# A fused attention and gated feed-forward kernel: k and q of half the batches turned by DMA transposes kept apart from the loads, unread matmuls in TensorE's first waits, and a new plan

## The chip, the cores and the metric

One core of one Trainium2 chip runs the whole program. The metric is the device time of one execution in microseconds (us). Each ratio below is between runs of the kernel before and a changed kernel on the same chip, in alternating rounds. Where two changed kernels from different rounds are compared by their medians, the chips differ too; the kernel before had 213.25 to 213.92 us in all of these rounds. Runs that the record marks as slow are named where they matter. In this kernel TensorE does the matmuls and writes them into PSUM, VectorE and ScalarE copy and compute elementwise, and GpSimd and SyncE issue the DMA transfers.

## The reference, cut to what matters

```python
batch, n_heads, seq, head_dim, n_pack = 8, 8, 576, 64, 32
p_packed = sm_attn(p, k, v)               # 32 packed queries attend over 576 keys
out      = sm_attn(q, p_packed, p_packed) # 576 queries attend over the 32 packed rows
x = out.transpose(0, 2, 1, 3).reshape(8 * 576, 512)
result = (((x @ w1) * (x @ w2)) @ w3) @ w_out      # float32, 4608 x 512
```

k and q come from memory with the sequence along partitions. Both attention steps contract over the head dimension, so k and q have to be turned. Of each batch there are 96 x 3072 values of k, of q and of v in fp16 after the load (589,824 bytes each).

## The kernel before: the parts that matter

The kernel is a list of operations. Each has the engines that may run it, an estimated duration and a priority. A list scheduler inside the kernel simulates the engines with these estimates and writes a fixed instruction order for each engine. On the chip each engine works through its own queue in that order, and semaphores only make it wait. An operation whose data comes later holds up whatever stands behind it on the same engine.

```python
def schedule(plan):
    ...
        dur = op.engines[e]
        if isinstance(dur, tuple):            # a DMA: time to issue, time to move
            issue, trans = dur
            free[e] = t + issue
            begin = max(free["DMA"], t + issue + 0.9)
            if begin < 11.0:
                trans *= 1.35
            free["DMA"] = begin + trans
            done[op], on[op] = begin + trans + LAG, "DMA"
    ...
    order.sort(key=lambda op: (start[op], op.n))
```

k and q are turned by TensorE, 24 transposes of 96x128 for one batch's k and 24 for its q, and two evictions of 128x1152 out of PSUM for each:

```python
def turned(which):
    ...
    for g in range(2):
        ps = Psum(2)
        for u in range(2):
            def fn(e, g=g, u=u, ps=ps):
                ...
                for hc in range(6):
                    ...
                    env.nc.tensor.transpose(t[:, u, SC*hc : SC*hc+SC], s[0:SC, h, 128*c3 : 128*c3+128], env.ident[0:SC, 0:SC])
        ...  # one copy to kT or qT by VectorE or ScalarE
```

v is copied by VectorE into a tile with a column of ones (`va`). All loads are issued from GpSimd's queue and are cast from float32 to fp16 on the way; the output is stored from SyncE's queue. kin, vin, qin, kT and qT have two buffers each, so batch b+2 reuses what batch b has finished with.

The softmax here doesn't subtract the row's maximum and nothing guards it: scores larger than these inputs give would overflow.

## Time and profile before

| | before |
|---|---|
| device time, median of 3 | 213.55 us (213.32 to 214.28) |
| span in the profile | 212.7 us |
| TensorE busy | 195.0 us, 92% |
| first matmul, last matmul ends | 9.02 us, 207.5 us |
| loads into SBUF, stores | 19.66 MB, 9.44 MB |
| loads arrive until about | 100 us, at some 200 GB/s; the last two, k7 and q7, are issued only at 111 and 137 us |

The prediction below shows the lines of the profile. "Granted clock" there is the share of its full clock that TensorE was given. "DMA share" is the time that the packets took, over the time of the core's 16 DMA engines; it passes 1 where packets overlap.

### The profile page before, as it was taken

To read this page: it belongs to the slowest core of one execution; us is meant where nothing else is said; L and a number is where in the kernel's file an instruction comes from. 1 tells how busy PE (TensorE), PEld (TensorE's weight loads), DVE (VectorE), ACT (ScalarE), POOL (GpSimd) and SP (SyncE) were. 2 spreads that over 40 slices of the span, in tenths; PEclk is the share of its full clock that TensorE was granted. 3 is DMA by queue.
4 is the path that set the end of the run, shared out by engine and by line. 5 is a ranking of instruction groups with operands and counts; after the bars stand their busy time and mean duration, and the time that the engine had idled before them with its cause. 6 is when DMAs were issued, how large, how long until landed. Compare 5 with 4: busy or idle time off the path is not lost.

```text
span 212.7 us, 6124 instructions
## 1 busy us (share of the span) xinstructions
PE 195.0 (92%) x2656; PEld 131.5 (62%) x2656; DVE 116.0 (55%) x188; ACT 137.0 (64%) x209; POOL 32.9 (15%) x49
## 2 busy tenths in 40 slices
PE   0188989999999999999999999999999999999990
PEld 0168878667567748785457766757755646776440
DVE  4015434367867776587946845447485665555100
ACT  2154749865798476986899555797858567555321
POOL 7742245511131112111000000100000000000000
PEclk9999999999999999999999999999999999999997
DMA  5999999999999999999829203192013313103353
GB/s 68 185 193 202 206 203 200 197 203 204 205 241 230 224 204 249 203 212 205 177 53 150 62 0 103 49 167 80 20 23 82 99 52 99 54 13 86 99 151 101
DMA packets 34124, 29.51 MB, mean 139 GB/s; under 512 B 3888, under 2 KB 28464, under 8 KB 34096
## 3 DMA queue, kind: packets, MB, share of 16 engines
q0 software_dynamic: 28336, 19.66, 62.7%
q1 hardware_dynamic: 5760, 9.44, 15.4%
q8 instruction: 21, 0.34, 0.6%
q14 instruction: 7, 0.06, 0.1%
HBM read 39.32 MB, written 9.44 MB: 229 GB/s over the span
## 4 chain that ended last, share of the span: by engine, by line
PE 89%; DMA 3%; ACT 2%; DVE 2%; issue 1%; POOL 0%; DVEq 0%; ACTq 0%; POOLq 0%
PE ps L585 29%; PE pb L624 29%; PE pb L365 8%; PE ps L412 7%; PE ps L557 5%; DMA ab<-in_moe_w_dram 3%; PE pb L445 2%; PE pb L468 2%; PE ps L534 2%; PE ps L624 2%; PE ps L514 2%; PE pb L347 1%; ACT ab L357 1%; PE ps L445 1%; DVE pT L334 1%
## 5 line engine op out<-in xcount | busy, mean ns | idle before, releaser
L585 PE MATMUL ps<-a,G 128*128 128x288 f16 x512 | 70.8, 286 | 0.2
L624 PE MATMUL pb<-wc,ab 128*128 128x512 bf16 x272 | 68.7, 380 | 0.0
L601 DVE TENSOR_TENSOR ab<-ps,bs 128x576 bf16<-128x576 f32 x64 | 48.2, 755 | 30.7 <-ACT bs L597 25.1
L585 PEld LDWEIGHTS <-G 128*128 128x128 f16 x512 | 48.5, 98 | 17.0 <-issue 0.9
L597 ACT CAST bs<-ps 128x576 bf16<-128x576 f32 x64 | 40.9, 639 | 26.5 <-PE ps L585 26.0
L624 PEld LDWEIGHTS <-ab 128*128 128x128 bf16 x288 | 25.8, 98 | 25.1 <-issue 2.7
L572 ACT CAST G<-ps 128x1024 f16<-128x1024 f32 x20 | 19.8, 1015 | 4.6 <-PE ps L557 4.4
L637 DVE COPY o<-pb 128x512 f32<-128x512 f32 x15 | 10.4, 691 | 20.7 <-PE pb L624 11.0
L639 ACT COPY o<-pb 128x512 f32<-128x512 f32 x19 | 11.1, 585 | 15.3 <-PE pb L624 15.0
L365 PE MATMUL pb<-wo,ab 128*128 128x256 f16 x128 | 16.7, 286 | 2.3 <-ACT ab L357 1.4
L570 DVE CAST G<-ps 128x1024 f16<-128x1024 f32 x12 | 14.4, 1221 | 3.2 <-PE ps L557 2.9
L365 PEld LDWEIGHTS <-ab 128*128 128x128 f16 x128 | 12.5, 102 | 5.2 <-ACT ab L357 2.7
L347 PE MATMUL pb<-ident,ab 128*128 128x128 f16 x48 | 4.8, 266 | 9.0 <-DMA ab<-in_moe_w_dram 9.0
L278 POOL DMA_DIRECT2D qin<-in_q_dram x8 | 6.2, 772 | 40.2 <-PE ps L412 34.2
L427 ACT COPY qT<-ps 128x1152 f16<-128x1152 f16 x9 | 10.0, 1117 | 3.4 <-PE ps L412 3.2
L540 ACT ACTIVATE ln<-ps 128x576 f32<-128x576 f32 x16 | 10.1, 650 | 2.7 <-PE ps L534 2.5
L557 PE MATMUL ps<-w,ppT 64*32 64x256 f16 x512 | 10.9, 272 | 0.1
L544 ACT ACTIVATE ri<-ln 128x576 f16<-128x576 f32 x16 | 10.7, 687 | 0.3
L456 ACT ACTIVATE es<-pb 96x512 f16<-96x512 f32 x18 | 10.4, 594 | 0.6
L347 PEld LDWEIGHTS <-ab 128*128 128x128 f16 x64 | 4.9, 116 | 9.4 <-DMA ab<-in_moe_w_dram 9.0
L357 ACT COPY ab<-pb 128x1024 f16<-128x1024 f16 x5 | 5.0, 1016 | 8.5 <-PE pb L347 8.5
L412 PE MATMUL ps<-ident,kin 96*128 96x96 f16 x192 | 10.3, 206 | 0.0
(56 smaller groups left out, 185.1 us busy)
## 6 DMA issues: line engine op xcount, KB each, us to landing
kin<-in_k_dram POOLq DMA_DIRECT2D x8, 576.0 KB, 13.6
vin<-in_v_dram POOLq DMA_DIRECT2D x8, 576.0 KB, 15.5
qin<-in_q_dram POOLq DMA_DIRECT2D x8, 576.0 KB, 15.5
out_dram<-o SPq DMA_DIRECT2D x24, 192.0 KB, 2.5
out_dram<-o SPq DMA_DIRECT2D x24, 128.0 KB, 2.4
ab<-in_moe_w_dram POOLq DMA_DIRECT2D x8, 256.0 KB, 10.2
w<-in_moe_w_dram POOLq DMA_DIRECT2D x8, 256.0 KB, 12.2
out_dram<-o SPq DMA_DIRECT2D x24, 64.0 KB, 2.2
```

Source lines behind the costliest of these rows:

```text
L347: env.nc.tensor.transpose(t[:, 128 * ct : 128 * ct + 128], env.w3[:, ci, 128 * ct : 128 * ct + 128], env.ident[:, :])
L365: env.nc.tensor.matmul(pv(ps)[:, 0:256], env.w3T[:, ci, 128 * ct : 128 * ct + 128], env.wo[:, h, ct, :], start=(ct == 0), stop=(ct == DFC ...
L412: env.nc.tensor.transpose(t[:, u, SC * hc : SC * hc + SC], s[0:SC, h, 128 * c3 : 128 * c3 + 128], env.ident[0:SC, 0:SC],)
L544: env.nc.scalar.activation(out=env.ri[g][:, :, :], in_=env.ln[g][:, :, :], func=AF.Exp, scale=-1.0)
L557: env.nc.tensor.matmul(pv(ps)[32 * hp : 32 * hp + 32, g, 256 * w : 256 * w + 256], env.ppT[b % 2][64 * g : 64 * g + 64, g, 32 * hp : 32 * ...
L570: env.nc.vector.tensor_copy(o, pv(ps))
L572: env.nc.scalar.copy(out=o, in_=pv(ps))
L585: env.nc.tensor.matmul(pv(ps)[:, half, 0:HS], env.G[b % 2][:, mc // 2, g, w, 128 * (mc % 2) : 128 * (mc % 2) + 128], env.a2[b % 2][:, g, h ...
L597: env.nc.scalar.copy(out=env.bs[bs][:, :, :], in_=pv(ps)[:, :, 0:HS])
L601: env.nc.vector.tensor_mul(env.ab(pair)[:, mc, b % 2, :].rearrange("p (a s) -> p a s", a=2), pv(ps)[:, :, 0:HS], env.bs[bs][:, :, :],)
L624: env.nc.tensor.matmul(pv(ps), ab[:, ic, 128 * t : 128 * t + 128], env.wc[:, ic, :], start=(ic == 0), stop=(ic == DFC - 1),)
L639: env.nc.scalar.copy(out=env.o[ob][:, :], in_=pv(ps))
```

## The change

The intent is to take 192 transposes (k and q of batches 4 to 7) from TensorE, which is the bound, to the DMA engines by `dma_start_transpose` on SyncE's queue. A list called `order` lays the loads and these transposes in groups, and semaphores make each group wait for the group ahead of it, so that a transpose never runs beside a load. Unread matmuls (their result is never used) on a small tile fill TensorE's waits up to 20 us so that its clock is at full rate when the first data come; the first loads come in another order; the planner's DMA estimates are new; and the priorities were searched again.

```diff
+    turn="k4 q4 k5 q5 k6 q6 k7 q7",
+    order="q2 k2 v2 k3 v3 q3 k4 q4 Tk4 Tq4 v4 k5 q5 Tk5 v5 k6 Tq5 q6 q7 Tk6 Tq6 v6 k7 v7 Tq7 Tk7",
+    warm=True,
-    T0=59.57,
+    T0=57.073,
     ... (the other priorities, also new)
-    loads="wo0 w33 w37 w36 pp w30 k_0 w34 wo1 v_0 q_0 w31 w35 k_1 ww0 w32 ww1 ww3 ww2 v_1 q_1",
+    loads="w37 pp w33 wo0 k_0 w36 wo1 w35 w34 w30 q_0 v_0 w31 w32 k_1 ww0 ww1 ww2 ww3 q_1 v_1",
 ...
-            issue, trans = dur
+            issue, lead, trans = dur
 ...                                    # planner: a load of k, q or v is now 2.9 us, a store 0.7, a transpose 2.7
+            if e == "PE" and warm and FILL_END > t > free[e] + FILL + 0.2:
+                ...                     # put groups of 8 unread matmuls where TensorE would wait
 ...
-            if by_dma:
+            if f"{which}{b}" in conf["turn"]:
                 def fn(e):
                     ...
-                    env.nc.sync.dma_start_transpose(
+                    return env.nc.sync.dma_start_transpose(
 ...
+    for i, name in enumerate(names):    # names from conf["order"]
+        if name[0] == "T":
+            gate_on = since_load        # a transpose waits for the loads since the last transposes
+        else:
+            gate_on = since_turn        # a load waits for the transposes since the last loads
+        op.gates = list(gate_on)
 ...
+            for p in getattr(op, "gates", ()):
+                tc.add_manual_dep(made[op].ins, made[p].ins.name, ..., reason="transposes apart from loads")
```

More of the change, by code (lines that the diff above doesn't have):

```diff
@@ L22 @@
 CONF = dict(
-    dma_from=8,
-    P=25.15,
-    T0=59.57,
-    lead=1.32,
-    at=dict(kT=-0.8, va=-0.14, s1=0.87, pv=0.59, ppT=-0.87, qT=-0.07, s2=0.43, z=0.51, G=0.14),
-    G_w=-0.01,
-    tg=[-30.99, -12.45, -0.15, 8.05, -11.49, -2.63, 7.81, -7.38, -17.47, 4.27],
-    ta=[-60.59, -5.81, -1.16, 6.18, -17.56, 4.69, -5.65, -11.68],
-    proj_off=0.87,
-    proj_w=0.98,
-    gate_w=0.03,
-    loads="wo0 w33 w37 w36 pp w30 k_0 w34 wo1 v_0 q_0 w31 w35 k_1 ww0 w32 ww1 ww3 ww2 v_1 q_1",
-    fold0=57.8,
-    fold1=3.02,
-    fold_w=3.51,
+    turn="k4 q4 k5 q5 k6 q6 k7 q7",
+    order="q2 k2 v2 k3 v3 q3 k4 q4 Tk4 Tq4 v4 k5 q5 Tk5 v5 k6 Tq5 q6 q7 Tk6 Tq6 v6 k7 v7 Tq7 Tk7",
+    warm=True,
+    P=25.1631,
+    T0=57.073,
+    lead=1.32,
+    at=dict(kT=-0.7408, va=-0.0681, s1=0.8793, pv=0.6033, ppT=-0.8967, qT=-0.1259, s2=0.3666, z=0.1937, G=0.1798),
+    G_w=0.0315,
+    tg=[-30.3628, -12.7069, -0.7448, 10.1275, -10.7998, -3.047, 4.5158, -7.7837, -17.0459, 6.4814],
+    ta=[-63.315, -4.0378, -0.4914, 4.9319, -18.4481, 6.6318, -9.5115, -11.1072],
+    proj_off=1.003,
+    proj_w=0.9994,
+    gate_w=0.1772,
+    loads="w37 pp w33 wo0 k_0 w36 wo1 w35 w34 w30 q_0 v_0 w31 w32 k_1 ww0 ww1 ww2 ww3 q_1 v_1",
+    fold0=58.7503,
+    fold1=-0.2625,
+    fold_w=4.1191,
 )
@@ L101 @@
 BEGIN, DMA_BEGIN, LAG = 1.27, 2.6, 0.6
+FILL, FILL_END, WARM_AT = 0.44, 20.0, 6.5
 def latency(a, b):
@@ L109, in latency, with schedule @@
     return LATENCY.get((a, b), 0.08)
-def schedule(plan):
+def schedule(plan, warm=CONF["warm"]):
     ops = plan.ops
@@ L146, in schedule @@
             push(op)
-    order = []
+    order, fills = [], []
     n_left = len(ops)
@@ L180, in schedule @@
         if isinstance(dur, tuple):
-            issue, trans = dur
-            free[e] = t + issue
-            begin = max(free["DMA"], t + issue + 0.9)
-            if begin < 11.0:
-                trans *= 1.35
+            issue, lead, trans = dur
+            begin = max(free["DMA"], t + lead)
+            if free["DMA"] == DMA_BEGIN:
+                trans += 1.5
+            elif begin > free["DMA"] + 0.5:
+                trans += 1.0
             free["DMA"] = begin + trans
+            free[e] = max(t + issue, begin + trans - 1.0) if e == "SP" and issue > 2 else t + issue
             done[op], on[op] = begin + trans + LAG, "DMA"
         else:
-            if e == "PE" and t < 4.0:
+            cold = e == "PE" and t < (WARM_AT if warm else 15.5)
+            if e == "PE" and warm and FILL_END > t > free[e] + FILL + 0.2:
+                spare = [i for i in range(len(slots) - 1, -1, -1) if slots[i] <= free[e]]
+                n = int((t - free[e] - 0.2) / (FILL * 2 if cold else FILL))
+                if spare and n:
+                    f = Op(op.n, "fill", {"PE": FILL}, plan.fill, 0.0, Psum(1))
+                    f.alloc.at, f.engine, f.repeat = spare[0], "PE", n
+                    start[f], done[f] = free[e], free[e] + n * FILL * (2 if cold else 1)
+                    fills.append(f)
+            if cold:
                 dur *= 2
@@ L204, in schedule @@
                 push(s)
+    order += fills
     order.sort(key=lambda op: (start[op], op.n))
@@ L219, in build_plan, with dma @@
     Ta = [T0 + P * (b - conf["lead"]) + d for b, d in enumerate(conf["ta"])]
-    rate = 0.199e6
-    def dma(nbytes, issue=0.77):
-        return (issue, nbytes / rate)
+    def dma(issue, trans):
+        return (issue, issue + 0.75, trans)
     def pv(p, n=512, dtype=FP32):
@@ L235, in build_plan, with load @@
     seq = [0]
-    def load(name, nbytes, fn, w, r=()):
+    def load(name, cost, fn, w, r=()):
         seq[0] += 1
-        return add("ld " + name, {"POOL": dma(nbytes)}, fn, -1000 + seq[0], w=w, r=r)
+        return add("ld " + name, {"POOL": cost}, fn, -1000 + seq[0], w=w, r=r)
     def load_w3(j):
@@ L243, in fn @@
             env.nc.gpsimd.dma_start(out=env.w3[:, j, :], in_=env.moe_w3[128 * j : 128 * j + 128, :])
-        load(f"w3 {j}", 128 * 1024 * 2, fn, [("w3", j)])
+        load(f"w3 {j}", dma(0.56, 1.25), fn, [("w3", j)])
     def load_wo(h):
@@ L251, in fn @@
             )
-        load(f"wo {h}", 1024 * 256 * 2, fn, [("wo", h)])
+        load(f"wo {h}", dma(1.0, 2.66), fn, [("wo", h)])
     def load_w12(qd):
@@ L260, in fn @@
                 )
-            load(f"w{w + 1} {qd}", 512 * 256 * 2, fn, [("w12", w, qd)])
+            load(f"w{w + 1} {qd}", dma(0.76, 1.34), fn, [("w12", w, qd)])
     def load_p():
@@ L269, in load_p @@
         seq[0] += 1
-        add("ld p", {"POOL": (1.16, 1.46)}, fn, -1000 + seq[0], w=[("pnat",)])
+        add("ld p", {"POOL": dma(1.17, 1.65)}, fn, -1000 + seq[0], w=[("pnat",)])
     def load_in(which, b):
@@ L277, in fn @@
             x = (env.k, env.v, env.q)[src]
-            env.nc.gpsimd.dma_start(
+            return env.nc.gpsimd.dma_start(
                 out=t[0:SC, :, :], in_=x[b].rearrange("h (p c) d -> p h (c d)", c=CK)
             )
-        load(f"{which}{b}", 96 * 3072 * 2, fn, [(which + "in", b % 2)])
+        load(f"{which}{b}", dma(0.78, 2.9), fn, [(which + "in", b % 2)])
     def emit_loads(names):
@@ L299, in consts @@
         nc = env.nc
-        nc.vector.memset(env.pT[:, :, :, :], 0.0)
         nc.vector.memset(env.blk[:, :], 0.0)
@@ L303, in consts @@
             nc.vector.memset(env.blk[32 * hp : 32 * hp + 32, 32 * hp : 32 * hp + 32], 1.0)
+        nc.vector.memset(env.pT[:, :, :, :], 0.0)
         for t in env.vaug:
@@ L387, in attention @@
     def attention(b):
-        by_dma = b >= conf["dma_from"]
         def turned(which):
@@ L401, in fn @@
                     )
-                add(f"{dst} {b}", {"SP": (1.0, 4.0)}, fn, att(b, dst) - 5, r=[(raw, b % 2)], w=keys)
+                add(f"T {which}{b}", {"SP": (2.9, 1.0, 2.7)}, fn, att(b, dst) - 5, r=[(raw, b % 2)], w=keys)
                 return
@@ L648, in fn @@
                     )
-            add(f"st {pair} {t}", {"SP": (0.3, 0.7)}, fn, vt + 0.9 * width / len(tiles), r=[("o", ob)])
+            add(f"st {pair} {t}", {"SP": (0.8, 1.0, 0.7)}, fn, vt + 0.9 * width / len(tiles), r=[("o", ob)])
     def rows_of(t, pair):
@@ L673, in build_plan, with fill @@
             project(pair, range(4, 9), Tg[b + 1], P * conf["proj_w"])
+    by_name = {op.name: op for op in plan.ops}
+    names = [("T " if x[0] == "T" else "ld ") + x.lstrip("T") for x in conf["order"].split()]
+    since_load, since_turn = [], []
+    last = None
+    for i, name in enumerate(names):
+        op = by_name[name]
+        if name[0] == "T":
+            if last != "T":
+                since_turn = []
+            gate_on = since_load
+            since_turn.append(op)
+        else:
+            op.vt = i - 500
+            if last == "T":
+                since_load = []
+            gate_on = since_turn
+            since_load.append(op)
+        last = name[0]
+        op.gates = list(gate_on)
+        for p in gate_on:
+            if p not in op.preds:
+                op.preds.add(p)
+                p.succs.append(op)
+    def fill(e):
+        for i in range(8):
+            env.nc.tensor.matmul(pv(fill.ps)[:, 0:128], env.blk[:, :], env.blk[:, :], start=True, stop=True)
+    plan.fill = fill
     return plan
@@ L765 @@
     )
+    made = {}
     for op in order:
-        if op not in first:
-            op.fn(op.engine)
+        if op.name == "fill":
+            op.fn.ps = op.alloc
+            for _ in range(op.repeat):
+                op.fn(op.engine)
+        elif op not in first:
+            made[op] = op.fn(op.engine)
+            for p in getattr(op, "gates", ()):
+                tc.add_manual_dep(
+                    made[op].ins,
+                    made[p].ins.name,
+                    mybir.DependencyInfo(mybir.DependencyClass.Sync, mybir.DependencyReason.DATA),
+                    reason="transposes apart from loads",
+                )
 _INS = ['q', 'k', 'v', 'p', 'moe_w1', 'moe_w2', 'moe_w3', 'moe_w_out']
```

## The prediction

> **What bounds the kernel now.** I read the page's busy shares first, then its chain that ended last, then the busy time by stretch, then TensorE's first 24 us instruction by instruction, and last the groups that the change removes.
>
> ```profile
> PE 195.0 (92%) x2656; PEld 131.5 (62%) x2656; DVE 116.0 (55%) x188; ACT 137.0 (64%) x209; POOL 32.9 (15%) x49
> ...
> PE 89%; DMA 3%; ACT 2%; DVE 2%; issue 1%; POOL 0%; DVEq 0%; ACTq 0%; POOLq 0%
> PE ps L585 29%; PE pb L624 29%; PE pb L365 8%; PE ps L412 7%; PE ps L557 5%; DMA ab<-in_moe_w_dram 3%; PE pb L445 2%; PE pb L468 2%; PE ps L534 2%; PE ps L624 2%; PE ps L514 2%; PE pb L347 1%; ACT ab L357 1%; PE ps L445 1%; DVE pT L334 1%
> ```
>
> TensorE is busy 92% of the span and is 89% of the chain. The transposes of k and q (L412) are 7% of the chain: 0.073 x 212.7 = 15.5 us for 384 of them. They are real TensorE time, not time beside something else. The next view says where TensorE's slack lies (busy time of TensorE by stretch, with clock, DMA share, GB/s):
>
> ```profile
> 0.00:9.02 9.02, 0.00 (x1) 1.00 0.79 115
> 9.02:19.26 10.24, 8.22 (x73) 1.00 1.45 196
> 19.26:50.00 30.74, 29.35 (x443) 1.00 1.34 202
> 50.00:207.50 157.50, 157.39 (x2144) 1.00 0.65 125
> ```
>
> From 50 to 207.5 us TensorE has no idle time (157.39 of 157.50). All idle time is early: 9.02 us before the first matmul, 2.02 us up to 19.26, 1.39 us up to 50. So two things can shorten the program: taking TensorE work out of the full stretch, which should count one for one, and a better start.
>
> ```profile
> 9.02 1.03 PE L347 MATMUL pb<-ident,ab 128*128 128x128 f16 x8 [9.02 <-DMA ab<-in_moe_w_dram]
> 11.16 1.89 PE L365 MATMUL pb<-wo,ab 128*128 128x256 f16 x8 [1.10 <-ACT ab L357]
> 12.84 1.91 PE L347 MATMUL pb<-ident,ab 128*128 128x128 f16 x16
> 15.00 2.25 PE L365 MATMUL pb<-wo,ab 128*128 128x256 f16 x16 [0.25 <-ACT ab L357]
> 17.09 0.61 PE L329 MATMUL pb<-ident,G 128*128 128x128 f16 x8
> 17.54 0.61 PE L347 MATMUL ps<-ident,ab 128*128 128x128 f16 x8
> ...
> 19.26 1.04 PE L365 MATMUL pb<-wo,ab 128*128 128x256 f16 x8 [0.66 <-DVE pT L334]
> ```
>
> The reader is to see the same instruction groups at two speeds. Eight transposes of w3 take 1.03 us at 9.02 and 0.61 us at 17.54; eight fold matmuls take 1.89 us at 11.16 and 1.04 us at 19.26. TensorE runs at half rate until about 15.6 us, although the granted clock is printed as 1.00 here: in this stretch the durations decide.
>
> **What the Trainium skill says.** "TensorE: Matmul & The Clock Gate", Part 1: The HAM clock gate: the default is half clock, and some 3.4 us of sustained activity releases it; 128 columns then go from 107 to 56 ns. The trace agrees on the sizes: (1.03 - 0.61) / 7 gaps is 60 ns by which the spacing shrinks. It took 6.6 us here, since the first matmuls have gaps of 1 us between them. The same page, Part 4: PE-mode transpose, says that transposes do not release the clock. The trace shows transposes at full rate once it is released (0.61 us for eight), and cannot say more; that the fill in the change is ordinary matmuls is the safe choice.
> "DMA: Bandwidth & Descriptors", Latency and other measured facts: a DMA transpose moves 261 GB/s, 350 to 400 in the contiguous case. "VectorE: DVE Perf Modes", The three transpose paths: one 128x128 transpose by DMA takes 1309 ns, by TensorE 390. These two give very different answers for a transpose of 96 x 3072 (24 blocks): 589,824 bytes / 261 GB/s = 2.3 us, or 24 x 1.309 = 31 us. No DMA transpose is in the trace of before, so it can't choose. I take the first, since the second looks like one small transfer with its fixed cost.
>
> **The change part by part.**
> (1) Removed on TensorE: k and q of four batches, 4 x 2 x 24 = 192 transposes.
>
> ```profile
> L412 PE MATMUL ps<-ident,kin 96*128 96x96 f16 x192 | 10.3, 206 | 0.0
> L412 PE MATMUL ps<-ident,qin 96*128 96x96 f16 x192 | 10.3, 206 | 0.0
> ```
>
> The 206 ns is the latency of one; they overlap. The chain of waits has them as "1.02 us x24", so 42.5 ns each on the path. 192 x 42.5 ns = 8.16 us. Of these all but a little lie after 75 us, where TensorE is never idle. Value: -8.2 us.
>
> (2) Removed on ScalarE and VectorE: 16 evictions of 128x1152 out of PSUM, at 1118 ns (ScalarE) or 756 ns (VectorE). Between 75 and 100 us ScalarE is busy 19.79 and VectorE 17.87 of 25 us, so neither was the bound. Value on the path: 0, some slack, and two-bank PSUM slots that come free sooner.
>
> (3) The start. The first load becomes one w3 block (262 kB) in place of half of w_out (524 kB) with a w3 block behind it. In the trace the loads brought 60 GB/s in the first 5 us and 188 GB/s in the next five, so the first 786 kB had been moved at 5 + (0.786 - 0.30) / 0.188 = 7.6 us, and the first matmul's data landed at 8.97, 1.4 us later. 262 kB are moved at about 4.8 us and land by the same distance at 6.2 us: the first useful matmul comes 2.8 us sooner. From there the loads set the pace until about 19 us. By the new order I get p at 7.6, the second w3 at 9.0, wo0 at 11.7, k0 at 14.8, w36 at 16.1 and wo1 at 18.7 us. The work that these make possible by 19.3 us is, at full clock: transposes of three w3 blocks 3 x 0.45, of p 0.9, three fold groups 2.94, k0's transposes 1.02, its scores 0.7, and 0.6 us of what wo1 opens: 7.5 us. Before, TensorE had done 8.22 us busy minus the cold excess (0.42 + 0.85 + 0.85 + 0.33 = 2.44 us from the rows above) = 5.8 us by that time. Difference: 1.7 us; after 19.3 us more work lies ready than before, so some of the 1.39 us of idle time there should go too. The unread matmuls serve this: they run where TensorE would wait, so at full rate they cost nothing, and they release the clock before the first real data. Without them much of the 2.44 us would return. They stop at 20 us. I count -2.0 us.
>
> (4) Added: eight DMA transposes on SyncE's queue. Each: 2.3 us of moving at the skill's rate plus about 2.2 us from issue to landing, which is what the smallest stores here take: an estimate of 4 to 4.5 us. None is on TensorE, so what matters is whether each lands in time. The gates make one chain of loads and transposes. k4 and q4 land when 13.8 MB are in, at about 200 GB/s and a start at 4.5 us: 73 us. Tk4 and Tq4: 81. v4, k5, q5 (8.9 us at that rate, 2 us latency): 92. Tk5 97. v5, k6: 105. Tq5 109. q6, q7: 117. Tk6, Tq6: 126. v6, k7, v7: 137. Tq7, Tk7: 146. Before, the scores of batch 7 began at 163.8 us; with some 10 us gained they should begin near 153. So the last has about 7 us of slack, the earlier ones 10 or more (scores of 6: 148 before, about 138 after, Tk6 122). Value: 0, if a transpose costs under some 5 us.
>
> (5) The gated loads leave holes in the DMA queues, and the stores share SyncE's queue with the transposes: small waits at most. I allow +0.4 us for new waits of this sort.
>
> Sum: 213.55 - 8.2 - 2.0 + 0.4 = 203.75 us; I say 203.5.
>
> **The rivals.**
> A. The transposes are slow. At 8 us each the chain above ends 30 us later, at about 176: TensorE runs out of other work and the time is near 225. At 31 us each it would be above 340. For: the 1309 ns figure, and that the planner had this path switched off before. Against: the bandwidth figure, and that the change plans each transpose in as few microseconds as a load. At 6 us each: 8 us of the slack are passed by some, about 206 to 210.
> B. Stores stuck behind a waiting transpose. SyncE issues in order; four output tiles are buffered. A transpose that waits 10 us for loads holds the stores, the output copies stop, a PSUM bank stays taken and TensorE stalls. For: the projections come in runs of a tile each 1.8 us around 55 to 60 us. Against: SyncE waited 121.1 us on ScalarE and 45.0 on VectorE, so it is idle most of the time, and over the span a tile comes each 4 us. If it bites: +1 to +4 us, so 204 to 207.
> C. The start gains nothing, as the loads are the limit there (share 1.45, 196 GB/s). Then only the removed work counts: 205.4.
> D. ScalarE or VectorE takes over as the bound in the denser stretch. They have 21% and 29% to spare between 75 and 100 us and lose work of their own, TensorE shrinks by 5%: I give it little; +1 us.
>
> **The range and the chances.** Sum 203.5; C alone gives 205.4, B or D some more; the start at its best (the earlier landing of 2.8 us and much of the cold excess, together 4.5 us) gives 201. So 8 times in 10 it lies between 200.5 and 207.0. Within 2% starts at 209.3, which needs rival A or several others together: faster 0.92, same 0.05, slower 0.03.
>
> **What would show it right or wrong.** (1) L412 has 192 matmuls instead of 384 and TensorE's busy time without the unread ones falls by about 8 us. (3) The first w3 transposes start near 6.2 us and take 0.6 us for eight. (4) A transpose takes 4 to 4.5 us from issue to landing, and no wait of TensorE on it is listed beyond a microsecond. (5) The stretch from 50 us to TensorE's end still has no idle time. The end after the last matmul stays 5.2 us. I am wrong if TensorE waits for kT or qT from a DMA, for output copies behind SyncE, or if the first matmul still waits until 9 us.

## The result, and the profile after

| | before | changed |
|---|---|---|
| device time, median of 4 | 213.92 us (213.32 to 214.89) | 222.15 us (220.72 to 223.17) |
| ratio | 1 | 1.0376, 95% interval 1.0302 to 1.0449 |
| span in the profile | 212.7 us | 220.0 us |
| mean granted TensorE clock | 0.994 | 0.977 |
| last matmul ends | 207.5 us | 215.7 us |

A ratio is the mean time of one kernel's runs over the mean of the other's runs in the same rounds, so it is not quite the ratio of the medians. Executions over 1.5% slower than the fastest of the same kernel are left out of the means. The result is correct; it is 3.8% slower where I had said 5% faster.

The page of the changed kernel, its busy shares and the chain of work that ended last (the line numbers have moved: L585 is now L597, L624 is L636, L601 is L613):

```profile
PE 197.2 (90%) x2568; PEld 131.2 (60%) x2568; DVE 111.3 (51%) x181; ACT 128.3 (58%) x200; POOL 33.0 (15%) x49
...
DMA 46%; PE 42%; POOL 3%; DVE 3%; issue 3%; ACT 1%; SPq 0%; POOLq 0%; ACTq 0%; DVEq 0%
```

The chain was 89% TensorE and 3% DMA; now it is 46% DMA. TensorE's busy 197.2 us contain 8.20 us of unread matmuls and, as is shown below, some 4.7 us (an estimate) by which half rate stretched its work, so its real work did shrink. What grew is waiting. Busy time of TensorE by stretch in the changed kernel (length, busy with count, granted clock, DMA share, GB/s):

```profile
0.00:20.00 20.00, 15.49 (x221) 1.00 1.13 153
20.00:50.00 30.00, 28.03 (x409) 1.00 1.33 202
50.00:75.00 25.00, 22.70 (x412) 1.00 1.29 222
75.00:100.00 25.00, 23.56 (x393) 1.00 0.91 165
100.00:125.00 25.00, 21.74 (x279) 0.86 0.78 147
125.00:150.00 25.00, 25.00 (x255) 1.00 0.87 161
150.00:175.00 25.00, 19.91 (x299) 0.93 0.96 160
```

The same stretches before have 8.96, 28.61, 25.00, 25.00, 24.89, 25.00 and 25.00 us busy. None of the removed transposes lies before 75 us in the kernel before (TensorE has done 144 of 384 by then, those of batches 4 to 7 being the last 192), so the sums up to there can be compared. Two things are to be seen. From 75 to 175 us the changed kernel idles 9.8 us (1.44 + 3.26 + 0 + 5.09), and twice the clock is below 1 in the stretch where it idles. And by 75 us, before the first DMA transpose is issued at 78 us, it is already behind: 66.2 us busy minus 8.2 unread is 58.0 us of work, while before has 62.6 us minus its cold excess of 2.4, which is 60.1.

The start itself looks as I had described it. TensorE's first instructions in the changed kernel (start, duration):

```profile
1.52 4.14 PE L714 MATMUL pb<-blk 128*128 128x128 f16 x40 [1.52 <-DVE blk L316]
5.50 0.61 PE L361 MATMUL pb<-ident,ab 128*128 128x128 f16 x8
...
8.73 1.07 PE L343 MATMUL pb<-ident,G 128*128 128x128 f16 x16 [1.73 <-DVE G L330]
...
12.52 1.91 PE L379 MATMUL pb<-wo,ab 128*128 128x256 f16 x16 [0.50 <-DMA wo<-in_moe_w_out_dram]
```

The first useful matmul is at 5.50 us instead of 9.02, and eight transposes take 0.61 us, the full rate. Still, by 20 us only 15.49 - 8.20 = 7.3 us of real work are done, 0.8 us more than before (8.96 - 2.44 = 6.5).

TensorE's two long waits are the longest ones of these two rows (who waited for whom, us in total, times, longest us; `ab` is VectorE's gate product, `va` its copy of v):

```profile
PE ps L597 <- DVE ab L613: 5.4, 4, 3.3
PE pb L480 <- DVE va L445: 3.9, 1, 3.9
```

Where the first of them comes from is in the chain between 89 and 127 us, in order of time (start, duration, what):

```profile
89.39 13.38 DMA qin<-in_q_dram
...
102.91 6.41 DMA kT<-kin
...
109.90 7.11 DMA vin<-in_v_dram
...
117.03 0.04 DVE va L445
...
117.90 0.76 DVE ab L613
...
118.70 1.12 PE ps L597 x4
119.82 0.43 PE pb L457 x8
120.25 2.88 PE ps L597 x12
```

Read it from the bottom. TensorE's gate matmuls start at 118.70, released by VectorE's gate product (`ab`), which frees their PSUM slot. The product had to wait behind the copy of v (`va`), which stands ahead of it in VectorE's queue; the copy waited for v5; v5 was issued only when the transpose of k5 had landed; and that one waited for the burst v4, k5, q5. In one line each, from who waited for whom (us in total, times, longest us), first the changed kernel:

```profile
DVE va L445 <- DMA vin<-in_v_dram: 12.6, 6, 4.3
```

and the kernel before:

```profile
DVE va L433 <- DMA vin<-in_v_dram: 0.7, 2, 0.4
```

The last line of the chain, 12 matmuls in 2.88 us where 12 take 1.47 us elsewhere, shows a second cost. Busy times and granted clock in a narrow stretch just after that wait (the columns are TensorE, its weight loads, VectorE, ScalarE, GpSimd, clock, DMA share, GB/s):

```profile
122.10:123.20 1.10, 1.10 (x17) 0.45 (x19) 0.76 (x1) 0.03 (x1) 0.00 (x0) 0.50 0.00 0
```

In stretches of 0.2 and 0.3 us the clock is 0.50 from 117.8 to 124.7 us, beginning within the wait of 3.26 us (115.44 to 118.70), and from 158.8 to 162.2 us, beginning 1.4 us after the end of the wait of 3.95 us (153.44 to 157.39). TensorE works at half rate for 6.0 and 3.4 us of these, and half of that, about 4.7 us, is an estimate of what it loses. So a long wait costs more than its own length. In the other runs too, each wait of 3.0 us or more after the start (3.02 and 5.99 us in after_nofill, 3.56 and 5.35 in v_ahead, 4.02 in turns_free) brings 3.4 or 6.8 us of half rate, and no shorter one does; the longest of those is 2.12 us, in tuned_gated.

With this the two traces can be balanced. Up to the last matmul (207.5 and 215.7 us), time without real work, idle or filled with unread matmuls, grew from 12.5 to 26.7 us (+14.2). Half rate took 4.7 us where the cold start had taken 2.4 (+2.3). What is left for the real work at full rate is 8.3 us less, as foretold; together +8.2.

How far the chain of loads and transposes ran from my estimate is best put in one table. "Measured" is when the next group was issued, at most 0.9 us after the one named had landed:

| group | predicted to land | measured |
|---|---|---|
| k4, q4 | 73 | 78 |
| transposes of k4, q4 | 81 | 87.9 |
| v4, k5, q5 | 92 | 102.9 |
| transpose of k5 | 97 | 109.9 |
| v5, k6 | 105 | 122.1 |
| transpose of q5 | 109 | 127.4 |
| q6, q7 | 117 | 137.1 |
| transposes of k6, q6 | 126 | 147.6 |
| v6, k7, v7 | 137 | 164.0 |

The reason is in the DMA engines' use between 120 and 132 us in the changed kernel (40 slices of 0.3 us, busy tenths and GB/s):

```profile
DMA  3100000000079999999970000000089169999999
GB/s 53 34 15 17 13 5 0 0 0 0 0 140 160 207 221 218 222 221 212 220 145 0 0 0 0 0 0 0 0 33 49 23 95 169 187 205 205 205 205 205
```

One transpose (of q5) moves in 10 slices, 3.0 us, at the rate of a load. On either side the engines stand nearly empty: some 3.3 us from the tail of the last load to the first packet of the transpose, and some 3.6 us from its last packet until the next loads flow. The gates make nine such hand-overs. Five show a pause of 2 to 3.6 us (the others of these at 77, 101 and 162 us); at the other four, stores and the tails of other transfers fall into it.

### The profile page after: what moved, and what is told of

Read it like the earlier page. It is cut to its first block, busy times and chain, and to the rows that moved or that the text cites. A ratio compares the mean times of both kernels' runs of the same rounds, so it can differ in the third digit from the quotient of the medians.

```text
span 220.0 us, 5956 instructions
## 1 busy us (share of the span) xinstructions
PE 197.2 (90%) x2568; PEld 131.2 (60%) x2568; DVE 111.3 (51%) x181; ACT 128.3 (58%) x200; POOL 33.0 (15%) x49
## 4 chain that ended last, share of the span: by engine, by line
DMA 46%; PE 42%; POOL 3%; DVE 3%; issue 3%; ACT 1%; SPq 0%; POOLq 0%; ACTq 0%; DVEq 0%
DMA vin<-in_v_dram 21%; PE ps L597 19%; PE pb L636 17%; DMA w<-in_moe_w_dram 7%; DMA ab<-in_moe_w_dram 6%; DMA qin<-in_q_dram 6%; DMA kT<-kin 3%; DMA qT<-qin 2%; PE ps L569 2%; PE ps L636 2%; DVE ab L613 1%; POOL ab L257 1%; DMA out_dram<-o 1%; PE pb L480 1%; POOL wo L262 1%
## 5 line engine op out<-in xcount | busy, mean ns | idle before, releaser
L597 PE MATMUL ps<-a,G 128*128 128x288 f16 x512 | 73.8, 293 | 6.2 <-DVE ab L613 5.4
L636 PE MATMUL pb<-wc,ab 128*128 128x512 bf16 x264 | 67.7, 384 | 0.0
L597 PEld LDWEIGHTS <-G 128*128 128x128 f16 x512 | 49.6, 100 | 24.8 <-issue 6.6
L613 DVE TENSOR_TENSOR ab<-ps,bs 128x576 bf16<-128x576 f32 x64 | 48.1, 755 | 30.7 <-ACT bs L609 26.1
L636 PEld LDWEIGHTS <-ab 128*128 128x128 bf16 x288 | 26.2, 98 | 26.1 <-issue 3.6
L584 ACT CAST G<-ps 128x1024 f16<-128x1024 f32 x18 | 18.0, 1013 | 4.8 <-PE ps L569 4.7
L582 DVE CAST G<-ps 128x1024 f16<-128x1024 f32 x14 | 16.7, 1221 | 3.6 <-PE ps L569 3.6
L292 POOL DMA_DIRECT2D vin<-in_v_dram x8 | 6.2, 772 | 74.5 <-DMA qT<-qin 23.9
L379 PE MATMUL pb<-wo,ab 128*128 128x256 f16 x120 | 14.4, 273 | 0.5 <-DMA wo<-in_moe_w_out_dram 0.5
L445 DVE COPY va<-vin 96x3072 f16<-96x3072 f16 x8 | 7.6, 954 | 12.6 <-DMA vin<-in_v_dram 12.6
L379 PEld LDWEIGHTS <-ab 128*128 128x128 f16 x128 | 11.9, 98 | 2.3 <-issue 0.6
L569 PEld LDWEIGHTS <-ppT 64*32 64x32 f16 x512 | 5.9, 91 | 7.8 <-issue 5.5
L537 ACT ACTIVATE es<-ps 128x576 f16<-128x576 f32 x16 | 9.7, 659 | 0.7 <-PE ps L526 0.7
L457 PEld LDWEIGHTS <-kT 128*128 128x128 f16 x192 | 8.0, 99 | 3.1 <-DMA kT<-kin 1.4
```

Source lines behind the costliest of these rows:

```text
L292: return env.nc.gpsimd.dma_start(out=t[0:SC, :, :], in_=x[b].rearrange("h (p c) d -> p h (c d)", c=CK))
L379: env.nc.tensor.matmul(pv(ps)[:, 0:256], env.w3T[:, ci, 128 * ct : 128 * ct + 128], env.wo[:, h, ct, :], start=(ct == 0), stop=(ct == DFC ...
L569: env.nc.tensor.matmul(pv(ps)[32 * hp : 32 * hp + 32, g, 256 * w : 256 * w + 256], env.ppT[b % 2][64 * g : 64 * g + 64, g, 32 * hp : 32 * ...
L582: env.nc.vector.tensor_copy(o, pv(ps))
L584: env.nc.scalar.copy(out=o, in_=pv(ps))
L597: env.nc.tensor.matmul(pv(ps)[:, half, 0:HS], env.G[b % 2][:, mc // 2, g, w, 128 * (mc % 2) : 128 * (mc % 2) + 128], env.a2[b % 2][:, g, h ...
```

## The experiments

Four theories and names are used in the expectations. G: the gates make v late, and its copy blocks VectorE. G2: the hand-overs make everything late, and v is only the first to be missed. P: what hurts is that the chain runs late against the instruction order that was laid out for it. The rivals are T (the transposes themselves cost), S (stores stuck behind transposes on SyncE's queue) and C (the chain is too long in any order). Where a figure has no range of its own here, it is the median of four runs; the kernel before had 213.25 to 213.69 us as median beside these.

### First round: the gates, the start, v, and half of the transposes

**no_gates.** The order of every engine is the changed kernel's; only the semaphores between loads and transposes are gone. Each transpose still waits for its own data.

```diff
-            for p in getattr(op, "gates", ()):
+            for p in ():
```

> The changed kernel with the same order of instructions on every engine, but without the added semaphores between loads and transposes. Theory G (the gates make the loads of v late, and the copies of v stand first in VectorE's in-order queue, so the gate products and then TensorE stop): v4 to v7 land 10 us and more earlier, TensorE's idle time from 50 us on falls from 12 us to under 4 us, and the time is 203 to 209 us. Rival T (the transposes themselves are the cost, and the gates protect them: beside loads each takes 10 us or more): k and q come late instead, TensorE waits for kT or qT, and the time stays at 218 us or above. Rival S (SyncE's queue: stores behind transposes): no change by more than 1%, as that queue keeps its order.

Measured: 210.78 us (209.38 to 211.59), ratio to before 0.9854, and correct. The gates alone cost 11.4 us, and without them the change is a gain of 1.5%. T falls. S had named a change of at most 1% and falls by its number; as the gates also hold SyncE's queue, the trace has to settle it: in the changed kernel output copies wait 1.8 us in all for a store to land (9.5 us before), and no wait of TensorE on an output copy is listed. The time is 2 us worse than G's range, though, and TensorE's idle time from 50 to 200 us fell from 12.1 to 5.1 us, not to under 4. v4 to v7 did land 14 to 27 us earlier. The transposes are slower beside loads. DMA issues of this run, median us from issue to landing:

```profile
kT<-kin SPq DMA_TRANSPOSE x4, 12.4
qT<-qin SPq DMA_TRANSPOSE x4, 7.0
```

In the changed kernel the medians are 6.4 and 4.9 us. So the gates do protect the transposes, and TensorE waited 1.8 us for a turned k here and 1.2 us more for another (a wait that the profile puts under VectorE, but that ends as the transpose of k7 lands). That protection is not worth its price.

**start_only.** The new start and the new priorities, nothing turned by DMA.

```diff
-    turn="k4 q4 k5 q5 k6 q6 k7 q7",
+    turn="",
     order=...  (the same without the T entries)
```

> The new order of first loads, the unread matmuls and the retuned priorities, with all of k and q turned by TensorE again and no gate. Theory G: nothing of the loss is in the start; TensorE's first useful matmul at 5.5 us at full rate; 211 us, that is before minus 2 to 3 us. If the retuned priorities or the start are themselves a cause: 214 us or above, with idle time of TensorE after 50 us.

Measured: 216.91 us (216.65 to 217.13), ratio 1.0148. This contradicts me: the start with its priorities loses 3.2 us where I had counted a gain of 2. TensorE's stretch from 50 to 75 us has 22.90 of 25 us busy, as in the changed kernel, with waits for k3 (1.3 us at 65 us) and for gate products behind copies of v (0.8 us; VectorE waits 2.4 us for v there).

**v_ahead.** All gates stay; v4, v5 and v6 move one burst ahead.

```diff
-    order="... k4 q4 Tk4 Tq4 v4 k5 q5 Tk5 v5 k6 Tq5 q6 q7 Tk6 Tq6 v6 k7 v7 Tq7 Tk7",
+    order="... k4 q4 v4 Tk4 Tq4 k5 q5 v5 Tk5 k6 Tq5 q6 v6 q7 Tk6 Tq6 k7 v7 Tq7 Tk7",
```

> All gates kept and eight transposes kept; only the loads of v4, v5 and v6 are moved one burst ahead of the transposes that held them. Theory G: the waits of VectorE for v (12.6 us in the changed kernel) shrink to under 4 us, but the chain of loads and transposes is as long as before, so k7 and q7 still come near 165 to 172 us and TensorE waits for them; 209 to 217 us, faster than the changed kernel by at least 2%. Rival T: within 1% of the changed kernel's 222 us.

Measured: 223.62 us (223.0 to 225.06), ratio 1.0472. Theory G in its first form falls (the number is where rival T had put it, but T had fallen with no_gates): VectorE's waits for v grew to 15.7 us in place of shrinking, and TensorE's longest waits are now these (who waited for whom, in this run):

```profile
PE ps L569 <- DVE ppT L513: 5.3, 1, 5.3
PE ps L636 <- DVE ab L613: 3.6, 1, 3.6
```

The planner laid the copies of v earlier too, to the new expected arrivals, and was late again by as much. Moving one kind of load within the chain doesn't shorten the chain.

**turn_67.** Only k and q of batches 6 and 7 are turned by DMA.

```diff
-    turn="k4 q4 k5 q5 k6 q6 k7 q7",
+    turn="k6 q6 k7 q7",
+    order="q2 k2 v2 k3 v3 q3 k4 q4 v4 k5 q5 v5 k6 q6 Tk6 Tq6 v6 k7 q7 v7 Tk7 Tq7",
```

> Only k and q of batches 6 and 7 turned by DMA, with their gates; 4 and 5 on TensorE again. Theory G: the chain has four transposes instead of eight and no load waits before 95 us; removed work 96 x 42.5 ns = 4.1 us, start 2.5 us: 207 to 210 us. Rival T: k6 to q7 late, 214 us or above.

Measured: 214.68 us (214.17 to 215.07), ratio 1.005. Against start_only it gains 2.2 us of the 4.1 us removed. By its number it lies in rival T's range (214 or above), but not for T's reason: no wait of TensorE on a turned k or q is listed. It decides little by itself, as the start's loss, which I had counted as a gain of 2.5 us, is in it too.

### Second round: which direction of the gates, and which part of the start

**loads_free.** A load no longer waits for transposes; a transpose still waits for the loads ahead of it.

```diff
-            for p in getattr(op, "gates", ()):
+            for p in (getattr(op, "gates", ()) if op.name[0] == "T" else ()):
```

> The changed kernel with half of its added semaphores: a transpose still waits for the loads listed ahead of it, but a load no longer waits for transposes. Theory G2 (the hand-overs: each time a load burst waits for a transpose to land, the DMA engines stand idle and the next loads come late; v is only the first to be missed): loads issue as in the run without any gate, transposes start later than there as each waits for more loads; 209 to 214 us, nearly all of the 11 us between gated and ungated comes back. Rival (both directions share the cost): 214 to 219 us.

Measured: 209.89 us (209.78 to 212.53), ratio 0.9854. All of the gates' cost is back.

**turns_free.** The other half alone.

```diff
+            for p in (getattr(op, "gates", ()) if op.name[0] == "l" else ()):
```

> The other half: a load still waits for the transposes listed ahead of it, a transpose waits only for its own data. Theory G2: the chain is as before, as a transpose's own data is mostly the last load of its burst; 216 to 222 us. Rival (the transposes' waits are the cost): 212 us or less.

Measured: 216.5 us, with a wide range (212.28 to 218.41). Three of the four runs count as slow, the profiled one too, so there is no ratio, and the one fast run, 212.28 us, is next to the rival's range and not in G2's. This run decides nothing. In its slow profile TensorE again waits 4.2 us for copies of v. What stands is loads_free: freeing the loads is enough. Whether freeing the transposes alone would do as much is open.

**before_warm.** The kernel before with 100 unread matmuls ahead of TensorE's first one, and VectorE's first `memset` moved behind those of the small tile (not shown); every other instruction in its place.

```diff
+            if op.name == "consts":
+                for i in range(100):
+                    nc.tensor.matmul(env.pairs[2][:, 0, 0:128], env.blk[:, :], env.blk[:, :], start=True, stop=True)
```

> The kernel before, every instruction in its order, with 100 unread matmuls of 128 columns put ahead of TensorE's first matmul (they end near 9 us, when the first data land) and the small tile that they read filled first. If the cold clock's 2.44 us were on the path: 211.1 us. If the loads set the pace of the start, as the kernel with the new start suggests: 213 to 213.7 us, the work is done sooner and TensorE waits longer; my bet is 213.0.

Measured: 214.47 us (214.33 to 214.54, six runs), ratio 1.0028, interval 0.9994 to 1.0062. The clock was at full rate: the first eight transposes took 0.62 us instead of 1.03. The time did not get shorter (it is 0.8 us above the range that I had given for this case). TensorE now reached its waits sooner: 2.2 us in all for ScalarE's copies of w3, and 0.8 us for q0. The cold clock was not on the path.

**start_b.** The new start with the old kernel's priorities.

```diff
     (start_only, with P, T0, at, tg, ta, fold0 and the like as before the change, and order=""; loads stays new)
```

> The new order of the first loads and the unread matmuls, with the priorities of the kernel before in place of the retuned ones, and everything turned by TensorE. If the retuned priorities cost the 3 us that the start-only kernel lost: 211 to 213.5 us. If the start itself (the new order of loads, or the unread matmuls up to 20 us) costs them: 215 us or above.

Measured: 218.44 us (218.07 to 218.94), ratio 1.0216. So the retuned priorities are not what costs. What start_only and start_b share is the order of the first loads, the unread matmuls and the planner's new DMA estimates. Either kernel's waits in the stretch 50 to 75 us are mostly for k3 and for gate products while VectorE waits for v (2.4 and 2.7 us), so for loads that come later than where the order puts their readers. Which of the three shared parts does it was not tried apart.

### Third round: the order laid out for the measured arrivals

By then the suspicion was theory P. The planner reckons with a store at 0.7 us of the DMA engines, but a tile of 256 KB at some 200 GB/s takes 1.3; it reckons with a pause costing 1.0 us. The next kernel differs from the changed one in these estimates alone. They change where instructions stand and, which the expectation overlooks, how many unread matmuls the planner puts in (176 in place of 104).

**replanned.**

```diff
-        load(f"{which}{b}", dma(0.78, 2.9), fn, ...)
+        load(f"{which}{b}", dma(0.78, 2.97), fn, ...)
-                trans += 1.0                        # first load after a pause
+                trans += 2.1
+            if begin < 16.0:
+                trans *= 1.12
-            add(f"st {pair} {t}", {"SP": (0.8, 1.0, 0.7)}, ...)
+            add(f"st {pair} {t}", {"SP": (0.8, 1.0, 1.25)}, ...)
-                add(f"T {which}{b}", {"SP": (2.9, 1.0, 2.7)}, ...)
+                add(f"T {which}{b}", {"SP": (2.9, 1.0, 3.3)}, ...)
```

> The changed kernel, gates and priorities and all, but the durations from which the kernel lays out its instruction order are set to what its own trace showed: a store 1.25 us of the DMA engines in place of 0.7, a transpose 3.3 in place of 2.7, 2.1 us more for the first load after a pause in place of 1.0, the loads of the first 16 us 12% longer, 2.97 us a load in place of 2.9. No semaphore and no byte differs; only what stands where in each engine's queue. Theory P (the chain of loads and transposes is late against the order that was laid out for it, so the engines stand before instructions whose data has not come while later ones could run): 207 to 213 us, and TensorE's idle time after 75 us is less than half of the changed kernel's 9.8 us. Rival C (the chain itself is too long, whatever the order): 218 us or above.

Measured: 213.86 us (212.91 to 214.71), ratio 1.0018. The gates, loads, transposes and stores are the same (the stores stand elsewhere among the transposes in SyncE's queue), and 8.3 us are gone; C falls. It misses P's range by 0.9 us. That the added unread matmuls do this is unlikely: without any, the changed kernel takes 222.13 us (after_nofill, below). VectorE's wait for v in this run (us in total, times, longest):

```profile
DVE va L447 <- DMA vin<-in_v_dram: 5.3, 5, 2.2
```

This is 5.3 us in place of 12.6, and not because the chain got faster. SyncE's last two transposes (start, time on the queue), first in the changed kernel, then in this run:

```profile
163.99 3.25 SPq L410 DMA_TRANSPOSE kT<-kin  x1
167.78 3.64 SPq L410 DMA_TRANSPOSE qT<-qin  x1
```

```profile
165.01 3.21 SPq L412 DMA_TRANSPOSE kT<-kin  x1
168.31 3.63 SPq L412 DMA_TRANSPOSE qT<-qin  x1
```

The chain is even a little later, and the kernel 8.3 us faster: what changed is what the engines had in their queues meanwhile. The idle time after 75 us did not quite halve by the stretches (1.4 us from 100 to 125, 2.3 from 150 to 175 and 1.3 from 175 to 200, together 5.0 against 9.8), but no wait is longer than 1.2 us, and the clock stays at 1, so the estimated 4.7 us of half rate are gone too. Part of the gain lies ahead of the chain: 24.11 us are busy from 50 to 75 us in place of 22.70.

**tuned_gated, tuned_nogate, tuned_start.** For these the priorities and the order of the first loads were searched with the corrected estimates (random steps, the planner's own end time as the measure). The first keeps all gates, the second has none in the plan nor in the program, the third turns everything on TensorE.

```diff
     (replanned, with other numbers in P, T0, at, tg, ta, fold0, loads; then)
 tuned_nogate:   order=""        and   for p in ():
 tuned_start:    turn="", order=""
```

> As the run before, and the priorities and the order of the first loads searched again with these durations. Theory P: 202 to 208 us, faster than both kernels with every gate still there. Rival C: 214 us or above.

> Eight transposes, no gate in the program or in its plan, measured durations, priorities searched again. Theory P: 203 to 208 us, no better than the gated one, as then both have an order that fits the arrivals. If the gates cost by themselves: 3 us or more below the gated one.

> The new start (unread matmuls, new first loads), everything turned by TensorE, measured durations, priorities searched again. If the start is worth what I predicted, 2 us: 211 to 212 us. If a sooner first matmul is worth nothing because the loads set the pace up to 75 us: 213 to 214.5 us, as before.

Measured: tuned_gated 212.16 us (210.4 to 213.46), ratio 0.9924; tuned_nogate 208.35 us (207.77 to 209.49), ratio 0.9768, interval 0.9731 to 0.9804; tuned_start 213.99 us (213.25 to 214.57), ratio 1.0023. The search gained little with the gates, outside P's range and short of C's: they seem to have a cost of their own, 3.8 us between the first two, though each was searched by itself and the luck of the search is in this. tuned_nogate beats both kernels, by 2.3% and 6.2%. And the new start shows no gain even with a fitting order (its stretch from 50 to 75 us is full again, 25.00 us). TensorE's stretches in tuned_nogate:

```profile
50.00:75.00 25.00, 24.99 (x401) 1.00 1.29 221
75.00:200.00 125.00, 123.94 (x1560) 1.00 0.93 149
```

It is full again from 50 us to its end at some 202 us. Its transposes take 11.9 us (k) and 10.3 us (q) to land beside loads, longer than in any gated run, and it doesn't matter, because their readers stand late enough.

### Fourth round: what was left open

**replanned_nosem.** The order of replanned, without the semaphores.

```diff
     (replanned) and
-            for p in getattr(op, "gates", ()):
+            for p in ():
```

> The replanned kernel's order on every engine, without the semaphores between loads and transposes. If gates and order are one cause (the chain late against the order), the order now fits a late chain and the time stays within 1% of the replanned kernel's 213.9 us. If the gates cost by themselves: 210 us or less.

Measured: 211.66 us (211.3 to 212.01), ratio 0.9914. This is between the two expectations. With it the square is complete (medians, us):

| | with the gates' semaphores | without |
|---|---|---|
| order of the change | 222.15 | 210.78 |
| order for the measured arrivals | 213.86 | 211.66 |

The semaphores cost 11.4 us with the first order and 2.2 us with the second. So most of their cost is the mismatch between the late chain and the order, and some 2 us (3.8 us between the two searched kernels) is the chain's own.

**after_nofill, best_nofill.** The unread matmuls taken out of the changed kernel and out of tuned_nogate.

```diff
         if op.name == "fill":
             op.fn.ps = op.alloc
-            for _ in range(op.repeat):
-                op.fn(op.engine)
+            pass
```

> The changed kernel without its 104 unread matmuls, all else the same. If they cost nothing and gain little: 221 to 223 us. If they stand in the way of real work: 220 us or less. If the warm clock were worth the 2.4 us of cold excess: 224 us or above.

> The fastest kernel so far (tuned_nogate, 208.35 us) without its unread matmuls. If the loads set the pace of the start: 208 to 209 us. If the warm clock counts: 210 us or above.

Measured: after_nofill 222.13 us (221.37 to 222.74), so nothing at all; best_nofill 210.89 us with a wide range (209.25 to 214.82); the run of 214.82 counts as slow, and the other three have 209.25, 210.16 and 211.63, ratio 0.9848 with an interval of 0.9774 to 0.9921, which overlaps with tuned_nogate's. Whether they are worth something in the fastest kernel is not settled. In best_nofill TensorE has 0.3 and 0.7 us of waits for turned k and runs the first groups at half rate (eight transposes in 1.04 us), and I can't say from two profiles which of it counts.

## Why the prediction was wrong, point by point

**Step 1, the removed transposes, -8.2 us.** The mechanism was right: the program has 192 such transposes instead of 384, and TensorE's real work at full rate shrank by 8.3 us in the balance above. Of the gain, 6.1 us came through between start_only (216.91) and no_gates (210.78), and 5.6 us between tuned_start (213.99) and tuned_nogate (208.35). The rest went into new waits, as far as pairs with different plans can say.

**Step 2, the evictions, 0.** Nothing contradicts it; VectorE is busy 51% of the changed kernel's span and ScalarE 58%, and the two long waits traced above come from VectorE waiting itself.

**Step 3, the start, -2.0 us: failed.** I had read the 9.02 us before the first matmul and the 2.44 us of half rate as time that the end would get back. The first useful matmul did come 3.5 us sooner and at full rate, but by 20 us this made 0.8 us more work where I had counted 1.7, and tuned_start gives 1.0023 and before_warm 1.0028. Of the 0.8 us, 0.2 are left at 50 us (35.3 us of work against 35.1) in a stretch where the loads move as fast as before (DMA share 1.33 and 202 GB/s in 20 to 50 us; 1.34 and 202 before). Rival C of the prediction ("the start gains nothing") named this. With the changed kernel's plan the start was even a loss of 3.2 us (start_only): TensorE stands 2.1 us in the stretch 50 to 75 us, which had been full. That the planner expects the loads too soon fits tuned_start, where the loss is gone, but new priorities came with it, so this cause is argued and not shown. Two readings in this step's background were loose: between 9.02 and 15.6 us TensorE has one gap of 1.10 us and one of 0.25, not several of 1 us, so why the clock took 6.6 us stays open; and the starts of the w3 transposes are 107 and 56 ns apart in the trace, a difference of 51 ns where (1.03 - 0.61) / 7 gave 60.

**Step 4, the transposes hidden, 0: failed, and it is the main error.** A single transpose was not far off: 4 to 4.5 us, measured 4.7 to 6.6 us with no load beside it. Rival A's slow transposes are not the cause, for when they are slower still (12.4 and 7.0 us, no_gates) the time is 210.78 us. What failed is the sum of the chain, "Tq7, Tk7: 146", measured at 172.7. I gave each load burst 2 us of latency and moved the loads at 200 GB/s. The chain was 5 us late before its first gate, lost 15 us more in its four bursts of loads and 6 us in the transposes. Five of the nine hand-overs leave the DMA engines nearly empty for 2 to 3.6 us, and the stores share the engines: from 87 to 103 us, 1.77 MB of loads and 1.00 MB of stores went through together, so that v4, k5, q5 took 15 us instead of 11. The second half of the error is that I compared these times with where the readers stood in the kernel before, and called 7 us slack. The readers' place is fixed by the new plan. It puts them where it expects the data, so that lateness becomes waiting, and an operation of VectorE that waits for v holds the gate products behind it.

**Step 5, +0.4 us for new waits: the term that was mis-sized.** It should have been about 11.4 us for the gates. Of these, 9.2 us (11.4 - 2.2) go away with an order that fits the late chain. The step named holes in the DMA queues, and they are there; what it left out is the wait for v on VectorE (12.6 us against 0.7) and the half rate after long waits.

In one row: 213.7 (before) + 3.2 (the start with its plan) - 6.1 (turned by DMA) + 11.4 (gates) = 222.2 us. Each term is the difference of two neighbouring runs, so the row has to add up and proves nothing by that.

**Rivals.** A had said that a chain ending at about 176 us gives near 225 us, and the chain ended at 172.7 with 222.15 us. That is luck: in replanned it ends just as late, with 213.86 us. B, the stores behind transposes, is not seen to matter: output copies wait 1.8 us in all for stores, and no wait of TensorE on them is listed. It was not tried by itself. D did not happen. The signs that I named were the right ones to look at: sign 5, no idle time from 50 us on, broke most clearly (12.1 us up to 200 us). Sign 4 broke in size: up to 6.6 us to landing, and a wait of TensorE of 1.14 us that ends as the transpose of k7 lands.

What stays open: which part of the start with its plan costs the 3.2 us, why start_b (old priorities) is 1.5 us worse than start_only, whether freeing the transposes alone would bring most of the gates' cost back too, and what the unread matmuls do in the fastest kernel.

## What to carry to other kernels

Where each engine's instruction order is fixed ahead of time, work that is moved to another engine pays in full only if the order is laid out for when its result really arrives; after any change to the transfers, put measured durations back into the plan before judging the change. Don't serialize transfers to make each of them fast if it is their chain that has readers: the transposes that took 12 us beside loads cost less than those that took 6 us with no load beside them. And a busy engine's late start is worth shortening only if its next data are there sooner too.

## What the Trainium skill lacked or had wrong

- "DMA: Bandwidth & Descriptors", Latency and other measured facts, gives a DMA transpose 261 GB/s or more. Here one of 589,824 bytes moved in 3.0 us, 197 GB/s, the rate of a load, and the eight landed 4.7 to 6.6 us after issue with no load beside them; SyncE's queue was taken for 2.9 to 3.6 us by each.
- "VectorE: DVE Perf Modes", The three transpose paths, has 1309 ns for one 128x128 transpose by DMA. It must not be multiplied: 24 blocks of 128x96 in one transfer took 4.7 us in all, 0.2 us a block.
- No page has what a transpose costs beside ordinary loads: medians of 12.4 us (k) and 7.0 us (q) to landing against 6.4 and 4.9 us when kept apart. The results stayed correct in every run without gates, which agrees with "DMA: Bandwidth & Descriptors", Rules for kernel authors, where a transpose next to ordinary DMAs needs nothing.
- No page has, as one figure, the price of making one group of transfers wait for another through a semaphore: 3.3 us from the loads' tail to a transpose's first packet and 3.6 us from its last packet to the next loads, with the DMA engines nearly empty, and 2 to 3.6 us at five of nine hand-overs.
- "TensorE: Matmul & The Clock Gate", Part 1: The HAM clock gate, has the idle time that lets the clock fall as one window of about 3.4 us, and that window as free-running. Here waits of 3.02 us (after_nofill) and 3.26 us were enough, so a window need not be idle from end to end. The free-running window agrees: the clock changed at 117.8, 124.7, 158.8 and 162.2 us, steps of about 6.8, 34.1 and 3.4 us, all multiples of 3.41, once inside a wait and once 1.4 us after one.
- No page has it that the granted clock is printed as 1.00 at the start of these profiles while the durations of the kernel before show half rate until 15.6 us.
